# Loading an eight-number vector once and spreading it with a product, and moving one load to another queue

## The chip, the cores and the metric

One core of one Trainium2 chip runs the whole kernel. The metric is the time of one execution on the device in microseconds (us). An execution with a profile also gives a *span*, some 1.7 us shorter than the time, and a trace of every instruction and transfer in it. All runs compared here are in the fast state, with a granted TensorE clock of 0.99 to 1.00; two single looks (c3 and c4) have no state of their own, because one run alone cannot be given one.

In the views, PE is TensorE (the matrix engine) and PEld its weight loads; DVE, ACT and POOL are the vector, scalar and GpSimd engines; SP only issues transfers. SPq and ACTq are the issuing of transfers on SP and on ACT, and their lists of transfers are called the SP and the ACT queue.

## The reference

Linear attention with a decay per head, followed by a two-layer network. In short:

```python
# q, k, v: (4, 8, 768, 64); lam: (8,), 0.97 to 0.99; block = 64
Dmask   = where(i >= j, lam ** (i - j), 0)
for each block b:
    out[b]   = ((qb @ kb.T) * Dmask) @ vb + (qb * lam ** (i + 1)) @ kv_state
    kv_state = lam ** block * kv_state + (kb * lam ** (block - 1 - j)).T @ vb
x = out.reshape(3072, 512)
h = x @ w_in                       # 512 -> 2048
return (h * sigmoid(1.702 * h)) @ w_out   # 2048 -> 512
```

So every use of q and k needs powers of `lam`, and these are the factors that the change gets at earlier.

## The kernel before

The kernel works through the sequence in windows of 128 positions. The first two windows are done in *units* (one pair of heads, half of the batch): load k, q and v, multiply k and q by the factors (`kqs`), turn them on TensorE (`ps_t`), scores (`ps_s`), mask, output (`ps_o`). Then the weights arrive and the *dense* products start (`ps_h` of w_in, `ps_out` of w_out). From then on the attention of the next windows is slipped in between dense products. The parts that matter here:

```python
def go(x):                                    # one load of k, q or v
    eng = nc.scalar if (w, nm, bl, p) == (0, "q", 0, 0) else nc.sync
    eng.dma_start(out=..., in_=SRC[nm][...])  # 128 KB or 256 KB, rows of 512 B
...
lam_p = const.tile([P, H], f32)               # 8 numbers on each of 128 partitions
nc.scalar.dma_start(out=lam_p, in_=bass.AP(..., ap=[[0, P], [1, H]]))
for bl, p, n in [(0, 0, 1), (0, 1, 2), (1, 0, 2), (1, 2, 2), (0, 3, 1)]:
    for nm in "kqv":
        load_units(0, nm, bl, p, n)
# then 16 pieces of w_in, 7 of w_out, the second window, the eighth of w_out ...
...
nc.scalar.activation(ln_lam, lam_p, LN)
nc.scalar.activation(kq_pow2[...], ln_lam, EXP, scale=kq_exp[...])    # four times
...
fill(FILL0)                                   # FILL0 = 12; products of zeros, to warm TensorE up
...
u_cast_kq(0, 0, *UNITS[0], nc.vector)         # k by its factors, on DVE
u_cast_kq(0, 1, *UNITS[0], nc.gpsimd)         # q by its factors, on POOL
for i in range(N + 2):                        # N = 8 units
    ...
    fill(FILL[i]); u_turn(0, *u)
    ...
    if i == N:
        for fc in range(NF):
            mlp1(0, fc, [0])                  # first products of w_in, between two units
```

## Time and profile before

| | before |
|---|---|
| time, median (range) | 213.38 us (213.01 to 213.98) |
| span of the profiled run | 212.0 us |
| TensorE busy | 206.3 us, 97% |
| lam lands / ln starts | 4.46 / 4.48 us |
| first casts of k / q | 5.50 / 5.93 us |
| dense products start | 19.27 us |

Landing times are read from the trace: a load has landed when the last of its engines has reported. The dense start is the start of the first run of at least eight products of w_in without anything between them.

The prediction shows the page's two rows, the chain of waits and the head of the timeline.

### The profile page before, as it was taken

Reading aid. Unit: us, or ns where it says so; the run is one execution under the profiler, and the core shown is the slowest. Engines: PE = TensorE matmul, PEld = TensorE weight load, DVE = VectorE, ACT = ScalarE, POOL = GpSimd, SP = SyncE. Lnnn points to the kernel's source line nnn. Section 1 sums busy time; section 2 is a strip of 40 time slices with the busy share of each in tenths; the row PEclk is TensorE's granted clock in tenths of the full one; section 3 lists DMA queues with packets and bytes.
Section 4 is the critical chain, followed back from the end, with each engine's and each line's share of the span. In section 5 each row is a group of like instructions: output and inputs, shape, how many; then the busy total and the mean of one; then the engine's idle time right before and its main releaser. Section 6 shows DMA issues by size and latency. Waiting matters only on the chain.

```text
span 212.0 us, 4433 instructions
## 1 busy us (share of the span) xinstructions
PE 206.3 (97%) x1758; PEld 108.0 (51%) x1758; DVE 105.1 (50%) x233; ACT 90.0 (42%) x182; POOL 31.6 (15%) x64
## 2 busy tenths in 40 slices
PE   7899999999999999999999999999999999999994
PEld 3464444457855865445554445554445544444443
DVE  5885645375678765276652637552655331100121
ACT  3886761247623752285320365420366320466000
POOL 6783000462004000004000060000130000000000
PEclk9999999999999999999999999999999999999999
DMA  5999999999996999999987999489881233100112
GB/s 134 302 327 367 299 394 382 313 287 205 233 270 129 192 233 178 231 253 208 190 197 161 283 209 197 99 179 214 213 164 27 53 86 116 50 0 0 49 53 99
DMA packets 95461, 40.15 MB, mean 189 GB/s; under 512 B 76880, under 2 KB 89424, under 8 KB 95440
## 3 DMA queue, kind: packets, MB, share of 16 engines
q1 hardware_dynamic: 95024, 39.73, 77.9%
q8 instruction: 14, 0.23, 0.5%
q10 hardware_dynamic: 416, 0.14, 0.2%
q14 instruction: 7, 0.06, 0.1%
HBM read 27.27 MB, written 6.29 MB: 158 GB/s over the span
## 4 chain that ended last, share of the span: by engine, by line
PE 74%; DMA 17%; DVE 4%; SPq 3%; issue 1%; ACT 0%; DVEq 0%
PE ps_out L539 32%; PE ps_h L511 30%; DMA ring<-in_moe_w_out_dram 7%; DMA ring<-in_moe_w_in_dram 6%; PE ps_o L486 3%; PE ps_s L449 3%; SPq L90 2%; DMA kq<-kqs 2%; DMA ring<-in_k_dram 2%; PE ps_out L554 2%; PE ps_kv L464 1%; PE ps_o L479 1%; DVE sm L325 1%; PE ps_t L298 1%; DVE kqs L280 1%
## 5 line engine op out<-in xcount | busy, mean ns | idle before, releaser
L511 PE MATMUL ps_h<-xT,w_in 128*128 128x512 bf16 (+1 forms) x448 | 86.5, 349 | 0.0
L539 PE MATMUL ps_out<-w_out,g_sb 128*128 128x512 bf16 x368 | 83.0, 379 | 0.1
L517 ACT ACTIVATE g_sb<-ps_h 128x512 bf16<-128x512 f32 (+1 forms) x112 | 58.5, 538 | 56.5 <-PE ps_h L511 55.2
L511 PEld LDWEIGHTS <-w_in 128*128 128x128 bf16 x448 | 42.9, 98 | 37.9 <-DVE w_in L157 0.2
L539 PEld LDWEIGHTS <-g_sb 128*128 128x128 bf16 x368 | 35.0, 98 | 40.1 <-issue 0.6
L546 DVE COPY o_sb<-ps_out 128x512 f32<-128x512 f32 x17 | 11.7, 691 | 51.0 <-PE ps_out L539 50.8
L456 DVE SCALAR_TENSOR_TENSOR sm<-ps_s,inv_pow,mask 128x512 bf16<-128x512 f32 x32 | 22.6, 747 | 23.7 <-PE ps_s L449 23.5
L489 ACT CAST xs<-ps_o 128x512 bf16<-128x512 f32 x16 | 9.4, 585 | 24.1 <-PE ps_o L486 24.1
L438 POOL CAST v_bd<-ring 128x512 bf16<-128x512 f32 x8 | 4.8, 644 | 55.8 <-DMA ring<-in_v_dram 55.8
L280 POOL TENSOR_TENSOR kqs<-ring,kq_pow 128x256 bf16<-128x256 f32 x14 | 8.8, 641 | 24.8 <-DMA ring<-in_q_dram 23.1
L325 DVE TENSOR_TENSOR sm<-ps_s,mask 128x512 bf16<-128x512 f32 x16 | 10.6, 686 | 3.1 <-PE ps_s L320 2.8
L436 DVE TENSOR_SCALAR kqs<-ring,q_pow 128x256 bf16<-128x256 f32 x32 | 10.4, 368 | 2.8 <-DMA ring<-in_q_dram 2.8
L468 DVE SCALAR_TENSOR_TENSOR kv<-kv,blk,ps_kv 64x256 bf16<-64x256 bf16 x24 | 11.4, 475 | 0.2
L438 POOL CAST v_sb<-ring 128x512 bf16<-128x512 f32 x8 | 5.5, 732 | 38.9 <-DMA ring<-in_v_dram 38.9
L436 DVE TENSOR_SCALAR kqs<-ring,k_pow 128x256 bf16<-128x256 f32 x32 | 10.9, 381 | 0.2
L157 DVE CAST w_out<-ring 128x512 bf16<-128x512 f32 x16 | 6.1, 424 | 6.5 <-DMA ring<-in_moe_w_out_dram 6.5
L280 DVE TENSOR_TENSOR kqs<-ring,kq_pow 128x256 bf16<-128x256 f32 x18 | 8.4, 495 | 1.6 <-ACT kq_pow L218 1.4
L544 ACT COPY o_sb<-ps_out 128x512 f32<-128x512 f32 x6 | 3.5, 586 | 12.2 <-PE ps_out L539 11.5
L271 PE MATMUL ps_f<-zeros 128*128 128x512 f32 (+3 forms) x14 | 7.5, 651 | 1.1 <-DVE zeros L187 1.1
L288 POOL CAST v_bd<-ring 128x256 bf16<-128x256 f32 x16 | 7.3, 483 | 2.4 <-DMA ring<-in_v_dram 2.4
L157 DVE CAST w_in<-ring 128x512 bf16<-128x512 f32 x13 | 5.6, 427 | 3.9 <-DMA ring<-in_moe_w_in_dram 3.9
L449 PEld LDWEIGHTS <-kq 64*128 64x128 bf16 x128 | 3.6, 94 | 6.7 <-issue 5.3
(71 smaller groups left out, 117.8 us busy)
## 6 DMA issues: line engine op xcount, KB each, us to landing
ring<-in_k_dram SPq DMA_DIRECT2D x23, 256.0 KB, 4.4
ring<-in_q_dram SPq DMA_DIRECT2D x23, 256.0 KB, 4.6
ring<-in_v_dram SPq DMA_DIRECT2D x23, 256.0 KB, 4.6
out_dram<-o_sb SPq DMA_DIRECT2D x23, 256.0 KB, 2.7
ring<-in_moe_w_in_dram SPq DMA_DIRECT2D x16, 256.0 KB, 6.1
ring<-in_moe_w_out_dram SPq DMA_DIRECT2D x8, 512.0 KB, 8.7
ring<-in_k_dram SPq DMA_DIRECT2D x2, 128.0 KB, 4.4
ring<-in_v_dram SPq DMA_DIRECT2D x2, 128.0 KB, 4.1
```

Of the source, the lines that this page charges most:

```text
L157: eng.tensor_copy((w_in_sb if kind == "in" else w_out_sb)[j][:, r, :], read(kind, j, r))
L280: eng.tensor_tensor(kqs_of[w, p][:, bl, i].rearrange("s j h d -> s h j d"), read(w, "kq"[i], bl, p), tab, op=MUL)
L325: nc.vector.tensor_tensor(sm.rearrange("s h j t -> s h (j t)"), s_ps.pop((w, bl, p))[:, :, 0 : 2 * P], mask2.to_broadcast([P, 2, 2 * P]), ...
L436: nc.vector.tensor_scalar(kqs[:, i, :, h, :], x[:, :, p, h, :], scalar1=(k_pow, q_pow)[i][:, 2 * p + h : 2 * p + h + 1], scalar2=None, op0 ...
L438: nc.gpsimd.tensor_copy(v_sb[w % 2][:, p], read(w, "v")[:, :, p])
L449: nc.tensor.matmul(s[:, h, b, :], t[hd(h), 0, b, :], t[hd(h), 1, b, :], start=True, stop=True)
L456: nc.vector.scalar_tensor_tensor(sm[:, h], s[:, h], inv_pow[:, 2 * p + h : 2 * p + h + 1], mask.to_broadcast([P, B, P]), op0=MUL, op1=MUL)
L468: nc.vector.scalar_tensor_tensor(new[hd(h), p], old[hd(h), p], blk2[hd(h), p : p + 1], t[hd(h), :, hd(h)], op0=MUL, op1=ADD)
L511: nc.tensor.matmul(t[:, bs[0] * P : bs[1] * P], w_in_sb[fc // CW][:, kc, :].rearrange("s (R m c) -> s R c m", R=2, c=2)[:, fc % CW // 2, f ...
L517: nc.scalar.activation(g_tile(w)[:, fc, c], h_ps.pop((w, fc))[:, c], GELU)
L539: nc.tensor.matmul(t, g_of[w][:, fc, g * P : (g + 1) * P], w_out_sb[j][:, fc % CW, :], start=(fc == 0), stop=(fc == FFC - 1))
L546: nc.vector.tensor_copy(o, t)
```

## The change

The intent: get the factors earlier, by replacing a load of 128 pieces of 32 B by a load of one piece and a product with ones that copies it to all partitions, and put the first q behind the first k in the SP queue instead of behind lam in the ACT queue. The fill of 12 x 128 columns becomes one of 4 x 128 ahead of the product and one of 5 x 128 behind it.

```diff
-            eng = nc.scalar if (w, nm, bl, p) == (0, "q", 0, 0) else nc.sync
-            eng.dma_start(
+            nc.sync.dma_start(
...
-    lam_p = const.tile([P, H], f32)
-    nc.scalar.dma_start(out=lam_p, in_=bass.AP(tensor=lam.tensor, offset=lam.offset, ap=[[0, P], [1, H]]))
+    lam_1 = const.tile([1, H], f32)
+    nc.scalar.dma_start(out=lam_1, in_=bass.AP(tensor=lam.tensor, offset=lam.offset, ap=[[0, 1], [1, H]]))
...
+    ones = const.tile([1, P], f32)
+    nc.vector.memset(ones, 1.0)
+    ps_lam = ps.tile([P, W], f32, tag="t", bufs=1, name="ps_lam")[:, 0:H]
+    with tc.manual_schedule():
+        fill(4)
+        nc.tensor.matmul(ps_lam, ones, lam_1, start=True, stop=True)
+        fill(5)
     ln_lam = const.tile([P, H], f32)
-    nc.scalar.activation(ln_lam, lam_p, LN)
+    nc.scalar.activation(ln_lam, ps_lam, LN)
...
-        fill(FILL0)
```

(`fill` itself moves up in the file, unchanged.)

## The prediction

> **What bounds the kernel now.** I read the page first, then the chain of waits, then the timeline of the first 20 us (the change touches nothing later), then the landing events of the single transfers in the trace.
>
> The page says that TensorE is busy nearly all the time, and that the DMA engines are saturated for the first half.
>
> ```profile
> PE 206.3 (97%) x1758; PEld 108.0 (51%) x1758; DVE 105.1 (50%) x233; ACT 90.0 (42%) x182; POOL 31.6 (15%) x64
> DMA  5999999999996999999987999489881233100112
> ```
>
> Only 212.0 - 206.3 = 5.7 us of TensorE are idle, and fills (products of zeros) count as busy. So the average does not tell what the start is worth. The chain of waits in its first 45 us does:
>
> ```profile
> 0.81 0.46 SPq L90
> 1.32 0.46 SPq L90
> 1.82 4.32 DMA ring<-in_k_dram
> ...
> 11.74 6.44 DMA ring<-in_moe_w_in_dram
> 18.19 5.23 DMA ring<-in_moe_w_in_dram
> 23.44 0.44 DVE w_in L157
> ...
> 23.93 15.81 DMA ring<-in_moe_w_out_dram x2
> 39.76 0.44 DVE w_out L157
> 40.24 1.58 PE ps_out L539 x6
> ```
>
> Columns are start and duration in us. Up to 40.24 us the chain is the SP queue and its transfers; after that it is nearly all TensorE. There is no lam, no ACT and no POOL in it. The landing events agree: the k loads of 256 KB and the q and v loads after them land at 6.14, 7.02, 7.92, 8.82, 9.74, 10.62, 11.55, 12.43, 13.34 us, one every 0.9 us (about 290 GB/s), without a gap. Then the weights follow, one of 256 KB each 0.65 us. This is a pipe that runs full from about 5 us on; whatever moves its whole stream moves the end.
>
> What happens ahead of that, in the timeline (start, duration, engine, line, what, and in brackets the idle time before and its releaser):
>
> ```profile
> 0.83 0.44 ACTq L164 DMA_DIRECT2D lam_p<-in_lam_dram  x1
> 1.12 4.33 PE L271 MATMUL ps_f<-zeros 128*128 128x512 f32 x6 [1.12 <-DVE zeros L187]
> 1.30 0.50 ACTq L90 DMA_DIRECT2D ring<-in_q_dram  x1
> 4.48 0.21 ACT L214 ACTIVATE ln_lam<-lam_p 128x8 f32<-128x8 f32 x1 [2.40 <-DMA lam_p<-in_lam_dram]
> 5.50 0.42 DVE L280 TENSOR_TENSOR kqs<-ring,kq_pow 128x256 bf16<-128x256 f32 x1 [1.39 <-ACT kq_pow L218]
> 5.93 0.61 POOL L280 TENSOR_TENSOR kqs<-ring,kq_pow 128x256 bf16<-128x256 f32 x1 [1.67 <-ACT kq_pow L218]
> 7.09 1.36 POOL L280 TENSOR_TENSOR kqs<-ring,kq_pow 128x256 bf16<-128x256 f32 x2
> 9.81 1.18 POOL L280 TENSOR_TENSOR kqs<-ring,kq_pow 128x256 bf16<-128x256 f32 x2 [0.68 <-DMA ring<-in_q_dram]
> 12.50 1.18 POOL L280 TENSOR_TENSOR kqs<-ring,kq_pow 128x256 bf16<-128x256 f32 x2 [0.62 <-DMA ring<-in_q_dram]
> ```
>
> The reader is to see two things. The first casts do wait for lam: it lands at 4.46 us, and the first k had landed at 4.63, the first q at 5.31. But this is repaid at once: the second q casts (7.09) start when their own data lands (7.02), and the third and fourth wait 0.68 and 0.62 us for q with POOL idle.
>
> **What the Trainium skill says.** (1) "DMA: Bandwidth & Descriptors", Specifications: transfers reach line rate from 512 B up; below that the engine reads, modifies and writes. The present lam load is 128 pieces of 32 B. The trace agrees that it is dear for its size: 4 KB took 3.6 us to land beside 4.0 for the 128 KB of q on the same queue. (2) The same page, "Issuing engines are not separate DMA queues": loads issued from different engines interleave on the same 16 DMA engines, and issuing from several saves only issue time. The trace agrees: with two queues active the first five loads moved 123 GB/s in the first 5 us, the single queue 305 in the next 5. (3) "TensorE: Matmul & The Clock Gate", Part 1: the array's clock is halved until about 3.4 us of activity. The trace agrees: weight loads of the first fills start at 2.13, 2.99 and 3.84 (0.86 apart for one 512-column pass of an f32 product), the next at 4.43 (0.59 later).
>
> **The change, part by part.** The order of instructions differs only at the head: SP gets q in second place, ACT loses it, lam is [1, 8], DVE gets one memset of ones, TensorE does fill(4), a product of ones with lam, fill(5) instead of fill(12). Everything after is the same.
>
> *Lam's path.* Removed: the wait to 4.46 us. Now one piece; in the trace the first of lam's 16 engines reported at 2.77 us, so I estimate landing at 2.8 to 3.1. Added: fill(4), two passes of 0.86 us from 1.12, ends at 2.84, so it is out of the way just in time. The product of 8 columns in f32 is two weight loads (0.24 us mean in the profile of fills) and two tiny passes: I estimate 0.5 us with its semaphore, so ln can start near 3.5 instead of 4.48, a gain of about 1.0. From the start of ln to the first k cast were 5.50 - 4.48 = 1.02 us, to the q cast 1.45. So the factors are ready at 4.5 and 4.95. That is just when k and q land, so the first casts go from 5.50 and 5.93 to about 4.65 and 5.05: 0.85 us earlier. fill(5), four passes, costs between 1.1 us (all warm) and 2.1 (all cold), so TensorE is free between 4.6 and 5.6, and the first transposes go from 5.98 to 5.1 to 5.6. All of this lies ahead of the next q landing (7.02 before), whose casts had started 0.07 us after it. So 0.07 us at most of the 0.85 can pass beyond unit 1, and none beyond the third q load. Worth at the end: 0.
>
> *The DMA stream.* Removed: 127 pieces. At the pipe's steady 300 to 330 packets in 0.5 us they are worth 127 / 630 = 0.20 us, and if each is a read-modify-write rather more. They sit in the poorest part: between 2.0 and 3.5 us the engines moved 75, 56 and 77 KB in each half microsecond, against 140 to 160 after 4 us. Moved: q from ACT to SP, so v and all later SP issues come one issue (0.46 + 0.05 us) later. Is this on the path? The second k was issued at 1.82 and its first packet is only at about 4.03, 2.2 us later, where the first k needed 1.1. So it stood behind others for 1.1 us, and 0.5 us later is still early enough. The first 256 packets of k last from 1.90 to 2.96, and q, issued at 1.32, can be there at 2.4 to 2.8. So a hole of at most 0.2 us. Issues from the ninth on wait for earlier landings anyway. Sum: -0.2 (pieces) -0.1 (read-modify-write, a guess within the range) +0.1 (half a hole) = -0.2; I say the stream lands 0.2 us earlier, k at 5.9 instead of 6.14.
>
> *The rest of the path.* With the stream go the weights, and with them the start of dense products at 19.27 us (w_in cast 18.85) and the wait for w_out at 40.24. After that TensorE runs dense and hands the 0.2 us through. 213.38 - 0.2 = 213.18; I put the prediction at 213.1, since what I am least sure of (the cost of small pieces) tends to the faster side.
>
> **The rivals.** (a) Lam's wait is on the path: the first casts' 0.85 us pass to the end, 212.5. For it: the three bracketed waits on kq_pow and lam. Against it: POOL waits of 0.68 and 0.62 us on q after, and no ACT in the chain up to there. (b) The SP queue is the bound in the ramp: the chain starts with three SP issues in a row. Then one more issue ahead costs its 0.51 us in full, and two queues no longer overlap in the slow ramp: 213.9. Against it: the 2.2 us from issue to first packet. (c) A new wait takes the place of the old one: lam's report stays behind the bytes of k on the same engines and comes at 4.4 after all. Then the product, ln and factors end near 5.9 for k and 6.4 for q, and fill(5) ends near 6.6, with TensorE cold again after a pause: 0.5 to 0.6 us later than now. POOL's slack ahead of the third q load is 0.68 us, so this would show in the first units and cost 0 to 0.2: 213.2 to 213.4. (d) Collisions: fetches of 16 KB of instructions fall among the loads at 14.85 and 21.41 us, and after the first the second w_in piece landed 2.1 us behind the first instead of 0.65. If the order on one DMA engine changes, this moves the dense start by a few tenths either way.
>
> **Range and chances.** All rivals stay within 212.4 and 213.9; the three runs of before alone span 0.97 us. I take 212.4 to 213.8. A change of 2% is 4.27 us, more than any rival makes; 0.99 for within 2%, the rest mostly for faster, as a hedge.
>
> **What would show it right or wrong.** Right: ln_lam starts between 3.3 and 3.8 us, waiting for TensorE; the first k and q casts wait for DMA or end within 0.3 us of its landing; the third q cast of POOL still waits for DMA; the second k lands 0.0 to 0.4 us earlier; the chain starts with the same SP issues and loads; w_in and w_out casts and the dense start shift by the same few tenths. Wrong: the second k lands later than 6.2 us (rival b), ln starts after 4.3 (rival c), the landings do not move but the dense products start 0.5 us earlier (rival a), or the landings shift and the end does not (d, or a wait late in the kernel that takes it back).

## More of the kernel before

One more view is needed for what follows: what TensorE waited for, with the sum, the number and the longest of the waits in us.

```profile
PE ps_f L271 <- DVE zeros L187: 1.1, 1, 1.1
PE ps_t L298 <- DVE kqs L280: 0.5, 1, 0.5
PE ps_s L449 <- DMA kq<-kqs: 0.4, 1, 0.4
PE ps_t L298 <- POOL kqs L280: 0.3, 1, 0.3
```

Three of the four belong to the head of the kernel. The third is the one that the prediction passed over: at 95 us, long after the change, TensorE waits for a transposing transfer of the fourth window.

## The result

| | before | changed |
|---|---|---|
| median of 5 runs | 213.38 us | 213.50 us |
| range | 213.01 to 213.98 | 213.32 to 214.06 |
| ratio, 95% interval | | 1.0011 (0.9988 to 1.0034) |

The ratio is the mean time of one kernel's fast runs over the mean of the other's of the same rounds, so it is not quite the ratio of the two medians. The interval does not even tell the sign.

The page's two rows that answer to those in the prediction look the same:

```profile
PE 204.7 (97%) x1737; PEld 108.6 (51%) x1760; DVE 104.8 (49%) x234; ACT 89.9 (42%) x182; POOL 33.1 (16%) x64
DMA  5999999998995999999999899489881233100112
```

TensorE's 204.7 us are not 1.6 us less work: 1737 products are on record beside 1760 weight loads, so some 23 records are missing from this trace (before, 1758 stood beside 1758).

That does not mean that nothing happened. The head of the changed kernel's timeline (start, duration, engine, line, what, and in brackets the idle time before it and its releaser), to be laid beside the lines that the prediction shows:

```profile
0.82 0.51 ACTq L163 DMA_DIRECT2D lam<-in_lam_dram  x1
1.31 0.45 SPq L89 DMA_DIRECT2D ring<-in_q_dram  x1
3.12 0.59 PE L226 MATMUL ps_lam<-lam,ones 1*128 1x8 f32 x2
3.75 0.18 ACT L229 ACTIVATE ln_lam<-ps_lam 128x8 f32<-128x8 f32 x1 [1.67 <-PE ps_lam L226]
4.75 0.43 DVE L287 TENSOR_TENSOR kqs<-ring,kq_pow 128x256 bf16<-128x256 f32 x1 [0.63 <-ACT kq_pow L233]
5.18 0.61 POOL L287 TENSOR_TENSOR kqs<-ring,kq_pow 128x256 bf16<-128x256 f32 x1 [0.92 <-ACT kq_pow L233]
6.41 1.36 POOL L287 TENSOR_TENSOR kqs<-ring,kq_pow 128x256 bf16<-128x256 f32 x2
9.71 1.36 POOL L287 TENSOR_TENSOR kqs<-ring,kq_pow 128x256 bf16<-128x256 f32 x2 [1.09 <-DMA ring<-in_q_dram]
12.42 1.18 POOL L287 TENSOR_TENSOR kqs<-ring,kq_pow 128x256 bf16<-128x256 f32 x2 [0.66 <-DMA ring<-in_q_dram]
```

The factors do come earlier: ln starts at 3.75 instead of 4.48, the first casts at 4.75 and 5.18 instead of 5.50 and 5.93. They still wait for the factors (the brackets name kq_pow), because the first k now lands at 3.00 and the first q at 3.73 instead of 4.63 and 5.31. Lam has landed at 1.99 us. (Its load leaves two updates in the trace, at 1.42 and 1.99, where that of 128 pieces leaves sixteen. By the Trainium skill, "DMA: Bandwidth & Descriptors", "Why a DMA increments its semaphore by 16 and not by 1", the issuing sequencer writes the share of the unused engines at once, without waiting for data, so only the last update means that the data is there.) So the product at 3.12 did not wait for it but for the fill ahead of it. The second pair of q casts is 0.68 us earlier (6.41 for 7.09), the third only 0.10 (9.71 for 9.81): there q is awaited, as before.

In this execution the gain is then lost, as the changed kernel's chain of waits shows (start and duration in us; a second profile, a1 below, looks different):

```profile
10.61 6.14 DMA ring<-in_moe_w_in_dram
...
16.81 0.62 POOL w_in L156
17.43 0.27 issue
17.70 0.59 PE ps_h L518 x2
...
20.09 3.35 PE ps_h L518 x15
23.48 9.23 PE ps_h L518 x42
32.71 1.51 PE ps_out L546 x7
```

The first piece of w_in lands at 16.75 us; before it was at 15.40. POOL casts it at once (16.81), and TensorE stands still for 1.1 us ahead of 17.70, since the products of that piece stand between two units in its order. So the dense products start at 20.02 us, 0.75 us *later* than before. The view of what TensorE waited for has that wait now, and the one of 95 us is gone:

```profile
PE ps_f L192 <- DVE zeros L186: 1.1, 1, 1.1
PE ps_h L518 <- POOL w_in L156: 1.1, 1, 1.1
PE ps_out L546 <- issue: 0.2, 1, 0.2
PE ps_out L546 <- PE ps_o L401: 0.2, 1, 0.2
```

A sum closes it. From starts of neighbouring products in the trace, less what the same pair takes where nothing is awaited (0.22 us between two dense products, 0.31 from a dense product to a score), TensorE before waited 0.35 us for the last piece of w_out at 40 us and 0.52 us for the transposes at 95 us; in the changed kernel both are zero. The dense start is +0.75, the waits are -0.35 and -0.52: together -0.12 us. The two spans differ by -0.15 (212.02 and 211.87).

### The profile page after: what moved, and what is told of

It is laid out like the page before. It is cut to its first block, busy times and chain, and to the rows that moved or that the text cites. A ratio compares the mean times of both kernels' runs of the same rounds, so it can differ in the third digit from the quotient of the medians.

```text
span 211.9 us, 4416 instructions
## 1 busy us (share of the span) xinstructions
PE 204.7 (97%) x1737; PEld 108.6 (51%) x1760; DVE 104.8 (49%) x234; ACT 89.9 (42%) x182; POOL 33.1 (16%) x64
## 4 chain that ended last, share of the span: by engine, by line
PE 86%; DMA 5%; SPq 4%; issue 1%; DVE 1%; POOL 0%; ACT 0%; DVEq 0%
PE ps_h L518 38%; PE ps_out L546 36%; SPq L89 4%; DMA ring<-in_moe_w_in_dram 3%; PE ps_o L493 3%; PE ps_s L456 3%; DMA ring<-in_v_dram 2%; PE ps_out L561 2%; PE ps_kv L471 1%; PE ps_o L486 1%; PE ps_t L305 1%; PE ps_o L401 1%; PE ps_s L327 0%; PE ps_o L392 0%; DVE kq L315 0%
## 5 line engine op out<-in xcount | busy, mean ns | idle before, releaser
L546 PE MATMUL ps_out<-w_out,g_sb 128*128 128x512 bf16 x354 | 80.7, 379 | 0.8 <-issue 0.2
L445 POOL CAST v_sb<-ring 128x512 bf16<-128x512 f32 x8 | 7.0, 916 | 37.6 <-DMA ring<-in_v_dram 23.7
```

Of the source, the lines that this page charges most:

```text
L445: nc.gpsimd.tensor_copy(v_sb[w % 2][:, p], read(w, "v")[:, :, p])
L546: nc.tensor.matmul(t, g_of[w][:, fc, g * P : (g + 1) * P], w_out_sb[j][:, fc % CW, :], start=(fc == 0), stop=(fc == FFC - 1))
```

## The experiments

The question is not where a large gain went, but what the two parts of the change did, and why neither an earlier nor a later start showed at the end. The same marks were read from every trace:

| execution | lam lands | second k lands | last v of window 1 | first w_in piece | dense start | wait at 40 us | wait at 95 us | span |
|---|---|---|---|---|---|---|---|---|
| before | 4.46 | 6.14 | 14.63 | 15.40 | 19.27 | 0.35 | 0.52 | 212.02 |
| before, again (c4) | 4.09 | 6.18 | 14.66 | 15.35 | 19.32 | 0 | 0.28 | 211.49 |
| changed | 1.99 | 5.49 | 14.72 | 16.75 | 20.02 | 0 | 0 | 211.87 |
| changed, again (a1) | 2.00 | 6.38 | 14.58 | 15.26 | 19.55 | 0 | 0.14 | 211.37 |
| lam part alone (a2) | 1.98 | 5.83 | 14.34 | 15.01 | 19.22 | 0 | 0.89 | 211.74 |
| lam part alone, again (c2) | 2.00 | 5.79 | 14.29 | 14.97 | 19.14 | 0.46 | 0.50 | 212.15 |
| q part alone (a3) | 3.99 | 6.64 | 14.99 | 17.18 | 20.44 | 0.51 | 0 | 212.78 |
| q part alone, again (c3) | 3.67 | 6.16 | 15.20 | 16.55 | 19.95 | 0 | 0.14 | 211.88 |

In all eight rows the span less dense start less the two waits is 191.6 to 192.1 us. So the end is fixed, to within half a microsecond, by three numbers: when the dense products start, and how long they then wait for transfers at 40 and at 95 us.

Another mark tells where the dense start comes from. In thirteen of the fourteen profiles the first scores (the first `ps_s`) start 1.82 to 2.15 us after the second k has landed, whether ln starts at 2.75 us (c1) or at 5.01 (b1). Only in b2, with ln at 5.73, is it 3.34. From the first scores to the dense start it is then 11.25 to 11.47 us in the seven profiles in which no piece of w_in is late and nothing is added (before, c4, a1, a2, c2, c1, b2). So, with factors no later than in the kernel before, the loads set the first scores, and earlier factors do not move them.

My theory after the result was: the lam part brings the loads forward, the q part holds them back, and what is left is taken up by the two later waits. The rivals: lam's wait is on the path; the early gain came from q in the SP queue; the first profile was an accident.

### a1: the changed kernel once more

No edit.

> The changed kernel once more, for a second profile and a firmer ratio. Theory (the early gain is real but is eaten at two places): the second k lands near 5.5 us (before: 6.14), the first fetch of 16 KB of TensorE instructions starts near 14.0 us (before: 14.85) and so meets the first piece of w_in, which lands near 16.7 (before: 15.40); the dense products start near 20.0 (before: 19.27); ratio 0.999 to 1.003. Rival (the collision in the first profile was an accident of that execution): the fetch starts anywhere between 13.5 and 15.5, w_in lands near 15.4, and the ratio is the same all the same.

Measured: median 213.25 us, ratio 0.9997 (0.9971 to 1.0024). The second k landed at 6.38 instead of 5.49, the fetch began at 14.24, w_in landed at 15.26. So the rival was right about the early k and about the late w_in of the first profile: each varies from execution to execution by 0.9 and 1.5 us. ln at 3.75 and the first casts at 4.74 and 5.17 were as in the first profile, but the first scores came at 8.24, where they had come at 7.45 (and at 7.97 in the kernel before): they went with the second k. What one profile shows of landings in the ramp must not be read as the change's effect.

### a2 and c2: the lam part alone

The first q stays on the ACT queue.

```diff
+            eng = nc.scalar if (w, nm, bl, p) == (0, "q", 0, 0) else nc.sync
-            nc.sync.dma_start(
+            eng.dma_start(
```

> The lam part alone: one piece of lam, the product with ones, the split fills; the first q stays on the ACT queue. The TensorE stream is that of the changed kernel. Theory: lam lands near 2.0 us, ln starts near 3.75, the second k lands 5.2 to 5.6 (the 127 small pieces are gone and the SP queue is not held up), the fetch comes near 14.0 and the dense start near 20.0; end as in the changed kernel, ratio 0.998 to 1.003. Rival (the gain of the early landings comes from q following k in one queue): the second k lands at 6.0 to 6.2 here.

> The lam part alone a second time, for the spread between executions and a firmer ratio. Theory (removing the small pieces lets the whole stream land 0.2 to 0.4 us earlier; the q part costs about as much): last v of the first window lands at 14.2 to 14.5 (before and its relatives: 14.61, 14.63, 14.75, 14.82), ratio 0.997 to 1.000. Rival (the earlier landings of the first lam-only run were chance): last v at 14.6 to 14.8.

Measured: ratios 0.9985 (0.9958 to 1.0012) and 1.0017 (0.9967 to 1.0066). (I had expected 0.997 to 1.000 of the second.) The second k landed at 5.83 and 5.79, between the 5.2 to 5.6 that I had expected and the rival's 6.0 to 6.2; the last v of the first window landed at 14.34 and 14.29, ahead of every kernel with the old lam load. The dense start near 20.0 that I expected did not come (19.22 and 19.14). The earlier stream is real, and it comes from the lam part (no run tells the load from the shorter fill in it), but neither time shows it: the dense start gained only 0.05 to 0.18 us on the two profiles of the kernel before, and TensorE waited 0.89 and 0.96 us later on, where that kernel waited 0.87 and 0.28. For a2, of TensorE's waits:

```profile
PE ps_s L457 <- DMA kq<-kqs: 0.8, 1, 0.8
```

Four of c2's six runs took 212.25 to 213.99 us and two 215.1; I have no profile of the longer ones, and why they are longer stays open.

### a3 and c3: the q part alone

Lam stays 128 pieces.

```diff
-            eng = nc.scalar if (w, nm, bl, p) == (0, "q", 0, 0) else nc.sync
-            eng.dma_start(
+            nc.sync.dma_start(
```

> The q part alone: lam stays 128 pieces of 32 B, fill(12) stays, q goes second in the SP queue. The TensorE stream is that of the kernel before. Theory: the second k lands at 6.2 to 6.7 (small pieces still in the ramp, SP half a microsecond later), the fetch comes at 14.8 to 15.3 and lets the first piece of w_in land first, dense start 19.2 to 19.8; ratio 0.999 to 1.004. Rival (q behind k is what brought the early landings): the second k lands near 5.5.

> The q part alone a second time, one look. Theory (one more issue ahead of the SP queue's loads costs 0.2 to 0.5 us of stream as long as lam's small pieces are there too): second k at 6.4 to 6.8, last v of the first window at 14.8 to 15.1. Rival (the late landings of the first look were chance): second k at 6.0 to 6.3, last v at 14.6 to 14.75.

Measured: ratio 1.0004 (0.9974 to 1.0034) for a3; c3 is a single look, 213.59 us. The second k landed at 6.64 and 6.16 (the second value in the rival's range). In a3 the fetch came at 14.23 and not at 14.8 to 15.3, the first piece of w_in landed late, at 17.18, and the dense products started at 20.44, past the 19.8 that I had allowed; this expectation failed. The last v landed at 14.99 and 15.20, later than in every kernel that leaves the head as it was. With that the stream's shift can be split. The last v of the first window landed at 14.69 us on average in the five profiles that leave the head of the loads alone (before, c4, a4, b2, b3: 14.61 to 14.82), at 14.26 in the three with the lam part alone (a2, c2, c1: 14.14 to 14.34), at 15.10 in the two with the q part alone, and at 14.56 in the three with both (changed, a1, b4: 14.37 to 14.72). So the lam part is worth -0.43 us, the q part +0.40, and both together -0.13. The ranges of lam part, old head and q part do not overlap; that of both together overlaps with the old head.

### a4: the first fill in twelve pieces

The kernel before, with 36 more instructions in TensorE's stream and the same columns.

```diff
-        fill(FILL0)
+        t0 = ps.tile([P, W], f32, tag="mm", bufs=3, name="ps_f")
+        for _ in range(FILL0):
+            nc.tensor.matmul(t0[:, 0:P], zeros, zeros[:, 0:1].to_broadcast([P, P]), start=True, stop=True)
```

> The kernel before, with its first fill of 12 x 128 columns as 12 products of 128 columns instead of 3 of 512: the same columns, 36 more instructions in the TensorE stream, no other change. Theory (the fetch is tied to the place in the TensorE stream, and where it falls decides when w_in lands): the first fetch comes 1.0 to 1.5 us earlier, at 13.4 to 13.9 us, the first piece of w_in lands at 16.4 to 16.9 instead of 15.40 and the dense products start 0.6 to 0.9 us later than 19.27, at 19.9 to 20.2; the time stays within 0.3% because later waits take that up. Rival 1 (the fetch is tied to time, or falls at random): it stays near 14.85 and the dense start near 19.3. Rival 2 (the dense start passes to the end): ratio 1.003 to 1.004.

Measured: ratio 1.0017 (0.9986 to 1.0049). The fetch began at 13.97, just later than I had said; w_in landed at 16.68 and the dense start was 19.94, as I had said. But the four profiles with the kernel before's own TensorE stream and no delay of it (before, c4, a3, c3) have the first fetch at 14.85, 14.33, 14.23 and 15.17, so it wanders by 0.9 us with no edit at all. The experiment does not separate my theory from chance: inconclusive. Two later runs speak against a fetch that is tied to time: b1 and b2 delay the same TensorE stream, and their first fetch comes at 18.29 and 16.59 us, behind 153 weight loads in both; in the other twelve profiles it comes behind 124 to 161.

### b1: two loads ahead of everything

```diff
+    for _ in range(2):
+        spare = op.tile([P, W], f32, tag="o", name="spare")
+        nc.sync.dma_start(out=spare..., in_=SRC["k"][3, 4:8, 2 * P : 4 * P, :]...)   # 256 KB, read by nobody
     pump()
```

> The kernel before with two loads of 256 KB that nobody reads at the head of the SP queue; nothing else changes. It delays the whole stream of loads. Theory (whatever moves the whole stream moves the end): the second k lands 1.4 to 2.0 us later than 6.14, at 7.5 to 8.1; all later landings and the last of w_out (39.74) shift by 1.4 to 2.0, and the end by 1.2 to 2.0, ratio 1.005 to 1.010. Rival (the stream has slack later on, so its shift is taken up): the landings shift but the ratio stays below 1.003.

Measured: median 215.58 us, ratio 1.0088 (1.0054 to 1.0121), that is +1.9 us. The second k landed at 8.44 (+2.30), the last v at 16.98 (+2.35), the last piece of w_out at 41.28 (+1.54), and the dense products started at 22.34 (+3.07). The landings moved more than I had expected, the time lies within the expected range. A shift of the whole stream towards later does reach the end. The theory holds, its rival falls.

Not all of the delay is the stream's, though. The profile (of the longest execution, span 214.6) has a stretch of half the granted clock from 8.52 to 11.93 us, after TensorE had stood still for 1.99 us (5.93 to 7.92). The first scores are 2.43 us late (10.40 for 7.97), about as late as the loads; the second unit's scores follow 2.09 us later, where all other profiles have 1.41 or 1.42, and that adds the rest of the 3.07. The three executions at a clock of 0.999 or more took 214.67, 214.72 and 216.18 us, still later than the 213.61 that the kernel before took on average in the same rounds.

### b2: lam's chain later

```diff
+    for i in range(6):
+        lam_q = const.tile([P, H], f32, name=f"lam_q{i}")
+        nc.scalar.copy(lam_q, lam_p)
+        lam_p = lam_q
     ln_lam = const.tile([P, H], f32)
```

> The kernel before with six copies of lam on ACT, one after the other, ahead of ln: the factors come about 1.8 us later (ln at 6.1 to 6.5 instead of 4.48), no transfer changes. Theory (lam's wait has about 0.7 us of slack ahead of the third load of q, and the start is paced by loads): the first casts come at 7.3 to 7.9, the first units shift by 1.5 to 2.0, POOL's wait for the third q (0.68) is gone, the last units shift by 0.3 to 1.2 and the dense start (19.27) by 0 to 0.8; ratio 0.999 to 1.003. Rival (a: lam's wait is on the path): the dense start and the end shift by 1.8 us, ratio 1.008.

Measured: ratio 1.0065 (1.0023 to 1.0107). ln came at 5.73 (+1.25, less than planned). No load was held back: the second k landed at 6.06, the last v at 14.61. Lines of its timeline:

```profile
5.73 0.21 ACT L218 ACTIVATE ln_lam<-lam_q 128x8 f32<-128x8 f32 x1
6.76 0.76 DVE L284 TENSOR_TENSOR kqs<-ring,kq_pow 128x256 bf16<-128x256 f32 x2 [2.64 <-ACT kq_pow L222]
9.40 0.31 PE L324 MATMUL ps_s<-kq 64*64 64x128 bf16 x8
10.30 1.36 POOL L284 TENSOR_TENSOR kqs<-ring,kq_pow 128x256 bf16<-128x256 f32 x2
10.81 0.31 PE L324 MATMUL ps_s<-kq 64*64 64x128 bf16 x8
12.41 0.31 PE L324 MATMUL ps_s<-kq 64*64 64x128 bf16 x8
```

POOL no longer waits for the third q (10.30 has no bracket), as I had expected. But the first scores of the units start at 9.40, 10.81, 12.41; before they started at 7.97, 9.38, 10.98. The distances are the same, 1.41 and 1.60, and they stay the same to the last unit, 1.44 us late (18.87 for 17.43). The dense start is 1.39 us late. The slack of 0.7 us that I had read from POOL's idle time is not there: the units follow one another in a rhythm of their own, and POOL's waits lie inside it. This step of the theory fell.

The times come in two groups, three runs of 213.9 to 214.3 and three of 215.7 to 216.3. The profile is of one of the first group, span 212.3: there the waits at 40 and 95 us are gone, which took up 0.87 of the 1.39. The groups differ in their granted clock: 0.998 to 1.000 in the first, 0.991 and 0.992 in the second. So the ratio of 1.0065 mixes two things. The first group alone is 0.5 us above the mean of the kernel before in the same rounds (214.08 and 213.61), a ratio of 1.002, which lies in the range that I had expected. The second group has no profile; its lower clock is what one stretch of half clock, as in b1 and b4, would give.

### b3: one more fill ahead of the dense products

```diff
             if i == N:
+                fill(4)
                 for fc in range(NF):
                     mlp1(0, fc, [0])
```

> The kernel before with one more fill of 4 x 128 columns (1.08 us of TensorE in its profile) just ahead of the first product of w_in; no transfer changes of itself. It delays the dense start by 0.7 to 1.1 us. Theory (later waits of TensorE on transfers, 0.35 us at 40 us and 0.5 us at 96 us, take it up): both waits disappear, the end moves by 0 to 0.4 us, ratio 1.000 to 1.002. Rival (TensorE is the path from the dense start on): the end moves by 0.7 to 1.1, ratio 1.0035 to 1.005.

Measured: ratio 1.0014 (0.9988 to 1.0041), that is +0.3 us by the ratio, +0.57 by the span. The dense products started at 20.64, 1.37 us late, more than the 0.7 to 1.1 that I had expected; but 0.45 of it was there before the fill (first scores at 8.42 for 7.97), so the fill itself added 0.92. Of TensorE's waits, the one at 95 us is halved, not gone:

```profile
PE ps_s L449 <- DMA kq<-kqs: 0.2, 1, 0.2
```

The wait at 40 us is gone. By the sum: +1.37 - 0.35 - 0.21 (0.52 to 0.31) = +0.81; the span less those three numbers is 191.6 here, at the low end of the band, which makes up the rest. A later dense start is in part taken up: the waits gave back 0.56 of the 1.37 us. The rival, which passes 0.7 us or more to the end, is not excluded, by the interval's upper end of 1.0041 or by this sum.

### b4: loads of the fourth window sooner

An attempt to take the wait at 95 us away, on the changed kernel.

```diff
-        load_spread(e + 1, 3, 1.5)
+        load_spread(e + 1, 3, 1.2)
```

> The changed kernel with the loads of the fourth window put 1.2 instead of 1.5 steps apart, so that its q loads (landed 84.1 to 89.4 us) are issued ahead of some transposes and stores; the numbers of the fourth window's transposes follow. If the wait of TensorE for the kq transposes near 95 us (0.15 to 0.9 us in the profiles so far) is what gives back an earlier start: the last q lands 1 to 2 us earlier, that wait is gone and the time falls by 0.2 to 0.6 us, ratio 0.997 to 0.999. Rival (another transfer takes its place, as the pipe is full until about 95 us): ratio 0.999 to 1.003.

Measured: median 216.86 us, ratio 1.0139 (1.0102 to 1.0176): 3 us slower. The last q landed at 88.47 instead of 89.42, less than hoped for, and the wait for kq is gone, but a longer one has taken its place:

```profile
PE ps_h L518 <- DMA xT<-xs: 2.2, 1, 2.2
```

The loads went ahead of the last transposing transfer of x in the SP queue. The changed kernel issues that transfer at 84.52 us, the edited one at 86.93, and TensorE has no dense work without it. The wait is not the whole loss in this profile. Its page, like that of b1, has a dip in the clock that TensorE was granted (the span in 40 slices, in tenths; first b4, then b1):

```profile
PEclk9999999999999999979999999999999999999999
PEclk9789999999999999999999999999999999999999
```

In b4 it is a stretch of half clock from 90.99 to 94.40 us, right after TensorE had stood still for 2.23 us (88.36 to 90.59). Dense products in it start 0.427 us apart instead of 0.216, eight of them, which costs 1.7 us. With that the sum closes against the changed kernel: dense start -0.52 (19.50 for 20.02), wait +2.4 (start to start), clock +1.7, together +3.6, where the spans differ by +3.4. One such stretch of 3.41 us in 214 is a mean clock of 0.992, as half of the executions of b1, b2 and b4 show and none of the others. The two profiled stretches come 0.4 and 0.6 us after TensorE had stood still for about 2 us, where no other profile has a pause over 1.1 us behind its first fill; that the pause is their cause is not shown, since the other half of the executions went without. Not all of b4's loss is the clock: its three executions at 0.998 or more took 215.34 to 217.19 us.

The queue is one line for loads, transposes and stores; what is moved forward moves something else back.

### c1: the lam part alone, with the product ahead of the fill

The rival's best case: lam landed at 1.98 us but the product stood behind a fill until 3.1.

```diff
     with tc.manual_schedule():
-        fill(4)
         nc.tensor.matmul(ps_lam, ones, lam_1, start=True, stop=True)
         fill(5)
```

> The lam part alone (first q on ACT), without the fill of 512 columns ahead of the product. In the lam-only run lam landed at 1.98 us but the product stood behind that fill until 3.1 and ln came at 3.76. Theory (earlier factors no longer pay, as loads set the pace): ln at 2.5 to 2.9, factors of k ready near 3.6, first k cast 3.5 to 3.8, first q cast at the landing of q (5.0 to 5.3), first transposes 4.4 to 5.0, first scores 7.0 to 7.8 (lam only: 7.82); dense start 18.7 to 19.3, the end within 0.15% of the lam-only kernel, ratio to before 0.996 to 1.000. Rival (a: lam's wait is on the path to the end): ratio 0.994 to 0.996, 1 us or more faster.

Measured: median 213.25 us, ratio 0.9992 (0.9957 to 1.0027). ln at 2.75, 1.7 us earlier than in the kernel before; first casts at 4.04 (later than the 3.5 to 3.8 expected) and 4.91, first scores at 7.55, dense start 19.02, the earliest of all. The wait at 95 us was 0.53 us, the span 211.43. The dense start is 0.25 us ahead of the kernel before's, but the second k also landed 0.54 us earlier than there (5.60), so even this cannot be put down to the factors; and the interval shows no time. No version is shown to beat both kernels.

### c4: the kernel before once more

No edit.

> The kernel before a second time, one look, for the spread. Theory: second k at 6.0 to 6.4 us, lam at 4.3 to 4.5, ln right after; whether the first fetch of TensorE instructions delays the first or the second piece of w_in depends on how far ahead of the last v's landing it starts: over 0.7 us ahead, the first piece lands near 16.7 and the dense start is near 20.0; under 0.4 us ahead, 15.4 and 19.3. Rival (the fetch has nothing to do with it): the pairing does not hold in this execution.

Measured: 213.29 us in a single look. The second k at 6.18, lam at 4.09, ln at 4.12, the fetch 0.33 us ahead of the last v, w_in at 15.35, dense start 19.32: as expected, but for lam, which was earlier than 4.3. Over all fourteen profiles, though, the rule fails twice. In c1 the fetch began 0.87 us ahead of the last v and the first piece landed in time (14.80); in c3 it began 0.03 ahead and the piece was late (16.55). What does hold better is this: in thirteen of the fourteen profiles, one of the 16 engines reports 0.5 to 1.7 us after the fifteenth, first on a load that lands within 3 us after the fetch's start, and on none between 9 us and the fetch (a4 does not show it so). Whether the first piece of w_in is caught may depend on which loads that engine still has ahead of it. That the fetch is the cause fits these times, but no run here shows it.

## Why the prediction was right or wrong

The time was right: 213.5 us lies in the range 212.4 to 213.8, and the main chance, within 2%, came true. The gain of 0.2 to 0.3 us that the prediction named is smaller than the interval (0.9988 to 1.0034), so no run confirms or refutes it. Its steps did not all hold, and two errors cancelled, which was luck.

**What bounds the kernel: half right.** A later stream of loads does move the end (b1). But the step "after that TensorE runs dense and hands the 0.2 us through" was wrong. The chain of waits of one execution is a path, not a statement that nothing lies beside it. TensorE waits again at 40 and at 95 us, 0 to 0.5 and 0 to 0.9 us by execution, and these waits tend to shrink when it comes later and to grow when it comes earlier (a2, b3 and the table).

**Lam's path: the worth was right, the reason in part.** Lam landed at 2.0 instead of the estimated 2.8 to 3.1, and it did not matter, because fill(4) held TensorE until 3.1 (estimate 2.84). ln at 3.75 and the casts at 4.75 and 5.18 lie within 0.25 us of the estimates. That k and q would land just then did not hold: they landed at 3.00 and 3.73, and the casts still waited for the factors. The first transposes, at 5.94, gained only 0.04, where 5.1 to 5.6 was said: fill(5) began at 3.65 and its 512-column passes were still 0.86 us long. How long they stay so varies: the distance of such passes falls from 0.85 to 0.43 us at about 4.2 us in the kernel before's first profile and at about 6.8 in its second. The worth at the end, 0, is what was found. In the first profile the first scores did move by 0.52 us (7.45 for 7.97) and those of the third unit by 0.38 (10.60 for 10.98), more than the 0.07 that the prediction lets pass; but the second k had landed 0.65 earlier, and in the second profile, with the same ln, it landed at 6.38 and the scores came at 8.24. So earlier factors pass nothing on, because the first scores wait for the second unit's loads. What fell is the reading of POOL's waits as slack: in b2 lateness went through undiminished to the last unit. From ln to the first scores it was 3.49 us in the kernel before and 3.67 in b2, so lam's chain and that of the loads ended almost together: earlier was worth nothing, later would have cost at once.

**The stream: the sum fitted by luck, both terms were too small.** I had -0.2 for the pieces, -0.1 for their read-modify-write, and +0.1 for the later issue. The runs show -0.43 for the lam part and +0.40 for the q part, which nearly cancel: -0.13 together, where I had said -0.2. The +0.1 counted half of a hole of 0.2 us; the whole issue (0.51 us) was nearer the truth, as rival b had it. Part of rival b was thus true, and the sum hid it. The -0.2 priced a piece of 32 B like a packet of 512 B; in the trace of the kernel before the 128 pieces took 7.8 ns each on average, and the 512-B packets of SP's queue in the first 6 us took 32. So the pieces' own time, 1.0 us on 16 engines, is under 0.1 us of the stream, and what makes up the 0.43 stays open. Where it starts is seen: the first k landed at 4.04 to 4.64 us in the seven profiles with 128 pieces (b1, with other loads ahead, left out) and at 2.90 to 3.07 in the six with one. The 123 against 305 GB/s that the prediction took as a sign that a second queue saves only issue time are no test of it, since no packet moved in the first 1.9 us; the q part is the test.

**The rivals.** (a) fell in its direction: factors 0.7 us earlier (changed) and 1.7 us earlier (c1) do not shorten the time. Lateness, though, moves the dense start in full (b2, 1.39 us), and half of b2's executions had a lower clock besides. (c) did not occur. (d), late pieces of w_in at the time of a fetch, came in the first profile and not in the second; the dense start was 0.75 us later with it, more than the "few tenths" that I had given it. Of the signs that I had listed as speaking against the prediction, "the landings shift and the end does not (d, or a wait late in the kernel that takes it back)" is what the lam part alone shows. The sign of rival b, a second k later than 6.2 us, came in one profile of the changed kernel (6.38) and not in the other (5.49), so it could not have decided anything.

## What to carry to other kernels

Before valuing an earlier start, list the later waits for transfers, not only the first: a start that comes earlier is worth nothing where the next wait grows by the same amount, while one that comes later may still cost. Take two parts of a change apart even when the sum is nil; here each part was worth 0.4 us of the stream of loads and they cancelled. Take a second profile of the same kernel before explaining half a microsecond in the ramp. And look at the granted clock of each execution before putting a microsecond down to a wait.

## What the Trainium skill lacked or had wrong

- "DMA: Bandwidth & Descriptors", Specifications, says that pieces under 512 B are slow, but not what a load of such pieces costs the loads beside it. Here 128 pieces of 32 B landed at 3.7 to 5.0 us and one piece at 2.0; the first k, on the other queue, landed at 4.04 to 4.64 us beside the 128 and at 2.90 to 3.07 beside the one, and the last load of the window came 0.43 us earlier (with the shorter fill, which no run separates).
- The same page, "Issuing engines are not separate DMA queues", calls the issue time saved by a second queue usually small relative to the transfer itself. That agrees (an issue of 0.46 us beside 4.0 us for the 128 KB of q), but it does not say that at the head of a kernel it can move everything behind: one load more in the SP queue came with a stream 0.40 us later, as much as the other part of the change gained.
- "Runtime: NRT & Kernel Launch", Instruction fetch mechanics, says that instructions are refilled in blocks of 16 KiB and that crossing a boundary is mostly hidden. The size agrees: the page of the kernel before has the row below (packets, MB, share of 16 engines), and the first fetch of each profile took 1.1 to 1.6 us. Not on the page is what a fetch does to the loads beside it: in thirteen of fourteen profiles one engine trailed the others by 0.5 to 1.7 us right after. In the changed kernel's first profile that came with a wait of 1.1 us on TensorE.

```profile
q8 instruction: 14, 0.23, 0.5%
```
